# Moving chunk 0's block transposes of g into chunk 1, and batch 1's mask onto TensorE

## The chip, the cores and the metric

The kernel runs on one core of a Trainium2 chip. The metric is the device time of one execution in microseconds. Five engines work from their own in-order instruction streams: TensorE (PE; its weight loads are shown apart as PEld), VectorE (DVE), ScalarE (ACT), GpSimd (POOL) and SyncE (SP), which here issues every DMA.

## The reference, cut to what matters

```
attn  = softmax(mask(0.125 * q @ k^T)) @ v        # 4 batches x 8 heads x 576 tokens x 64
                                                  # heads 0-3: the last 32 positions; heads 4-7: every 32nd position
x     = attn as [2304, 512]
h     = x @ w_in                                  # w_in [512, 2048], stored as 64-bit floats
g     = h * sigmoid(1.702 * h)
x2    = g @ w_out                                 # w_out [2048, 512], stored as 64-bit floats
logits = x2 @ phi                                 # 32 slots
d     = softmax over tokens; slot_in = d^T @ x2
slot_out[e] = relu(slot_in[e] @ w1[e]) @ w2[e]    # 8 experts
out   = softmax over slots (logits) @ slot_out
```

## The kernel before

The 2304 tokens are worked in five chunks (four of 512, one of 256), each in 16 steps, one for each 128 columns of h. `moe_step(i)` writes step (c, f): it brings the weights on, advances the side work (the generators in `side`), issues block transposes of g, and calls `gemm1`, where twelve matmuls make h (L319), ACT makes tanh (L322) and DVE makes g (L323). g lies in slots of 512 columns: 19 in the tile `gT` and, from chunk 1 on, three more in `more`. The logits are taken from g every four steps (L338). At the chunk's end `post(c)` makes the softmax weights d and multiplies them with g (128 small matmuls, L433, result `us`). For that product g is needed with its 32x32 blocks transposed: `g_transpose` (L346, on DVE) reads a slot and writes into place f of `gT`, and `todo` lists what is still to be transposed.

Chunk 0 is different from the others: its 16 steps also bring in the weights. Each step converts two 512 KB tiles of 64-bit floats to 32 bits. `load_raw` (L248) fetches a tile into one of three `raw` buffers; ACT takes the absolute value (L259), POOL clamps (L260), DVE does three bit operations (L261, L262, L263), the last of which frees the buffer. `split` makes the two halves of a weight (ACT L270, POOL L271). For w_out there are also four PE transposes (L278), a store to a scratch (L275) and a product with phi (L288, L294).

The attention of batch 0 runs ahead of chunk 0. That of batch c+1 is side work of chunk c, one piece a step (two in step 0): `att_scores` (scores L161, mask, maximum L174, exponentials L179 with a sum each, L180 to L182), `att_transpose` and `att_values` (L216). For batch 0 (`early`) TensorE adds the mask into PSUM as a matmul with the identity (L154), and the maximum (L174, then a small multiply L176) and the exponentials read PSUM. For the other batches DVE adds the mask on the way from PSUM to SBUF (L164). Scores, weight transposes and most other small products share a pool of five PSUM tiles (`mtile`).

The program's text sets priorities only. A planner in the tile framework orders each engine's instructions ahead of the run, by what is ready in its own account; on the chip each engine then runs its list in order.

Of the kernel before, what the change touches and what calls it, by code (L numbers as in the profile page):

```python
# [30 lines left out]
NF = FF // 128  # L31
TFROM = 5
# [9 lines left out]
def tile_kernel(ctx: ExitStack, tc: tile.TileContext, lqk, lv, sqk, sv, wraw, phi, wexp, cst, out):  # L42
# [22 lines left out]
    def mtile(name):  # L65
        return ps_m.tile([P, 512], F32, tag="m", name=name)
# [61 lines left out]
    def att_scores(b, hp, part):  # L128
        t = qkv[b, hp]
        local = hp < 2  # L130
        nk, step = (KL, QT) if local else (KS, QS)
        ko = S if local else SW
        total, half = (NTL, 5) if local else (NTS, HS)
        u0, u1 = (0, half) if part == 0 else (half, total)
        nt = u1 - u0
        early = b == 0
        nm = f"{b}_{hp}_{part}"
        if part == 0:
            shape = [P, NTL if local else 2 * HS, nk]
            if b == 0 and hp >= 2:  # L140
                ts = ep.tile(shape, F32, name=f"ts_{b}_{hp}")
            else:
                ts = att.tile(shape, F32, tag="ts", name=f"ts_{b}_{hp}")
            probs[b, hp] = ts
            if not local:
                nc.gpsimd.memset(ts[:, NTS], 0.0)
        if local:
            ts = probs[b, hp][:, u0:u1]
        else:
            ts = probs[b, hp].rearrange("p (j e) k -> p e j k", e=2)[:, part, :nt]  # L150
        sp = mtile(f"s_{nm}")[:, :nt * nk].rearrange("p (u k) -> p u k", k=nk)
        mask = maskL if local else maskS
        if early:
            nc.tensor.matmul(sp, identb, mask.unsqueeze(1).to_broadcast([P, nt, nk]), start=True, stop=False)  # L154
            if local and part == 0:
                nc.tensor.matmul(sp[:, 0], identb, maskL0, start=False, stop=False)
        for u in range(nt):
            qo = step * (u0 + u)
            for h in range(2):
                hs = slice(64 * h, 64 * h + 64)  # L160
                nc.tensor.matmul(sp[hs, u], t[hs, qo:qo + 64], t[hs, ko + qo:ko + qo + nk], start=not early, stop=not early or u == nt - 1)  # L161

        def add_mask(a, z, m):
            nc.vector.scalar_tensor_tensor(ts[:, a:z], sp[:, a:z], SCALE, m.unsqueeze(1).to_broadcast([P, z - a, nk]), op0=ALU.mult, op1=ALU.add)  # L164

        if not early:
            if local and part == 0:
                add_mask(0, 1, maskL0)
                add_mask(1, nt, mask)
            else:  # L170
                add_mask(0, nt, mask)
        nmx = att.tile([P, 6], F32, tag="nmx", name=f"nmx_{nm}", bufs=4)
        src, sc = (sp, SCALE) if early else (ts, 1.0)
        nc.vector.tensor_reduce(nmx[:, :nt], src, axis=AX.X, op=ALU.max, negate=True)  # L174
        if early:
            nc.vector.tensor_scalar_mul(nmx[:, :nt], nmx[:, :nt], SCALE)  # L176
        sm = att.tile([P, 6], F32, tag="sm", name=f"sm_{nm}", bufs=4)
        for u in range(nt):
            nc.scalar.activation(ts[:, u], src[:, u], AF.Exp, scale=sc, bias=nmx[:, u:u + 1], accum_out=sm[:, u:u + 1])  # L179
        nc.vector.tensor_scalar_add(sm[:, :nt], sm[:, :nt], 1e-9)  # L180
        nc.vector.reciprocal(sm[:, :nt], sm[:, :nt])  # L181
        nc.gpsimd.tensor_tensor(ts, ts, sm[:, :nt].unsqueeze(2).to_broadcast([P, nt, nk]), op=ALU.mult)  # L182
# [68 lines left out]
    def load_w(f):  # L251
        for k in range(2):
            if (f, k) not in raws:
                load_raw(f, k)
        for k in range(2):
            raw = raws.pop((f, k))
            t = rawp.tile([P, 512], F32, tag="wc", name=f"wc_{f}_{k}", bufs=4)
            u = t.bitcast(U32)
            nc.scalar.activation(t, raw[:, :, 1].bitcast(F32), AF.Abs)  # L259
            nc.gpsimd.tensor_scalar(t, t, F64_LARGE, F64_SMALL, op0=ALU.min, op1=ALU.max)  # L260
            nc.vector.tensor_scalar(u, u, 3, 0x3FFFFFF8, op0=ALU.logical_shift_left, op1=ALU.bitwise_and)  # L261
            nc.vector.scalar_tensor_tensor(u, raw[:, :, 1], 0xC0000000, u, op0=ALU.bitwise_and, op1=ALU.bitwise_or)  # L262
            nc.vector.scalar_tensor_tensor(u, raw[:, :, 0], 29, u, op0=ALU.logical_shift_right, op1=ALU.bitwise_or)  # L263
            conv[f, k] = t

    def split(f):
        if f % 2 == 0:
            wis[f // 2] = wip.tile([P, 2, 2, 512], F32R, tag="wi", name=f"wi_{f // 2}")
        w, t = wis[f // 2][:, f % 2], conv.pop((f, 0))
        nc.scalar.copy(w[:, 0], t)  # L270
        nc.gpsimd.tensor_tensor(w[:, 1], t, w[:, 0].bitcast(F32), op=ALU.subtract)  # L271

    def wo_transpose(f):
        t = conv.pop((f, 1))
        nc.sync.dma_start(wo_scr[f], t)  # L275
        tp = mtile(f"wot_{f}")
        for kt in range(4):
            nc.tensor.transpose(tp[:, 128 * kt:128 * kt + 128], t[:, 128 * kt:128 * kt + 128], ident)  # L278
        woT[f] = rawp.tile([P, 4, 128], F32, tag="woT", name=f"woT_{f}", bufs=1)
        nc.scalar.copy(woT[f].rearrange("p k f -> p (k f)"), tp)  # L280
# [3 lines left out]
    def wo_phi(f):  # L284
        t = woT.pop(f)
        pw = mtile(f"wp_{f}")[:, :P]
        for kt in range(4):
            nc.tensor.matmul(pw[32 * kt:32 * kt + 32], phs[:, kt, :], t[:, kt, :], start=True, stop=True)  # L288
        wpT[f] = rawp.tile([P, P], F32, tag="wpT", name=f"wpT_{f}", bufs=2)
        nc.scalar.mul(wpT[f], pw, 0.5)  # L290

    def wo_phi_sum(f):
        pw = mtile(f"wq_{f}")[:, :NS]
        nc.tensor.matmul(pw, wpT.pop(f), sel, start=True, stop=True)  # L294
        nc.scalar.copy(wp[:, f, :], pw)  # L295
# [3 lines left out]
    slots, taken, where = {}, set(), {}  # L299

    def g_slot(c, f):
        k = next(k for k in [*range(NF, NF + 6), NF - 2, NF - 1] if k in slots and k not in taken)
        assert k >= NF or c == 0
        taken.add(k)
        where[c, f] = k
        return slots[k]
# [5 lines left out]
    def gemm1(c, f):  # L312
        N = CHUNKS[c][1]
        x, w = xt[c], wis[f // 2][:, f % 2]
        h = ps_h.tile([P, 512], F32, tag="h", name=f"h_{c}_{f}")
        n = 0
        for kt in range(4):
            for we, xe in ((0, 0), (0, 1), (1, 0)):
                nc.tensor.matmul(h[:, :N], w[:, we, 128 * kt:128 * kt + 128], x[xe][:, kt, :N], start=n == 0, stop=n == 11)  # L319
                n += 1  # L320
        g = g_slot(c, f)
        nc.scalar.activation(g[:, :N], h[:, :N], AF.Tanh, scale=0.851)  # L322
        nc.vector.scalar_tensor_tensor(g[:, :N], g[:, :N], 1.0, h[:, :N], op0=ALU.add, op1=ALU.mult)  # L323
        gs[c, f] = g
# [16 lines left out]
    def g_transpose(c, f):  # L341
        N = CHUNKS[c][1]
        if c < 4:
            assert f not in taken
            taken.add(f)
        nc.vector.transpose(t_slots(c)[:, f, :N], gs[c, f][:, :N])  # L346
        g_used(c, f)

    gt = []
    side, st, todo = [], {}, []  # L350

    def moe_step(i):
        c, f = steps[i]
        if i + 2 < NF:
            load_w(i + 2)
        if 0 < i < NF:
            wo_phi(i)
        if i <= NF and i:
            wo_phi_sum(i - 1)
        for s in list(side):  # L360
            if next(s, True):
                side.remove(s)
        if i + 1 < NF:
            split(i + 1)
        if c == 0 or f >= TFROM:
            for _ in range(1 if c == 0 else 2):
                if todo and (c or todo[0][1] not in taken):
                    g_transpose(*todo.pop(0))
        while todo and todo[0][0] < c and todo[0][1] not in taken:
            g_transpose(*todo.pop(0))  # L370
        gemm1(c, f)
        if i + 1 < NF:
            wo_transpose(i + 1)
        if i and f % 4 == 0:
            pc, pf = steps[i - 4]
            logits(pc, pf)
            if f == 0:
                side.append(post(pc))
        todo.append((c, f))

    def post(c):
        N = CHUNKS[c][1]
        ntt = N // 128
        first, last = c == 0, c == len(CHUNKS) - 1
# [35 lines left out]
        nc.scalar.copy(L[:, :ntt], lp[:, :N // 4].rearrange("p (t s) -> p t s", s=NS))  # L420
        st["L"] = L
        yield
        if not last:
            yield
        us = [mtile(f"u_{c}_{a}") for a in range(4)]
        nb = N // 32
# [1 line left out]
        for i in range(nb // 4):  # L428
            for a in range(4):
                for j in range(4):  # L430
                    b = 4 * i + j
# [141 lines left out]
    c = len(CHUNKS) - 1  # L573
# [4 lines left out]
    for _ in post(c):  # L578
        pass
# [148 lines left out]
    for half in range(1, len(COLS)):  # L728
        todo = list(PARTS)
# [75 lines left out]
```

## Time and profile before

| | us |
|---|---|
| Median of 3 runs (441.43 to 441.65) | 441.59 |
| Profiled execution, its own time | 442.75 |
| Span of the profiled execution | 441.0 |
| DVE busy in the span | 264.9 (60%) |
| PE busy in the span | 410.5 (93%) |
| ACT / POOL busy in the span | 195.3 (44%) / 78.5 (18%) |
| Chunk 0, from about 35 to 145 us | 110 |
| Chunk 1, from about 145 to 217 us | 72 |
| Chunk 2, from about 217 to 288 us | 71 |

Busy shares are means over stages that have different limits, and ends of matmuls are modelled, so a busy PE need not be a PE at its peak. The slices of the page (each digit is the busy share in tenths of one fortieth of the span) show DVE at 8 or 9 from slice 4 to slice 11, which is chunk 0, and at 4 to 6 after it. The granted TensorE clock is at full speed in all but the last slices.

### The profile page before, as it was taken

To read this page: it belongs to the slowest core of one execution; us is meant where nothing else is said; L and a number is where in the kernel's file an instruction comes from. 1 tells how busy PE (TensorE), PEld (TensorE's weight loads), DVE (VectorE), ACT (ScalarE), POOL (GpSimd) and SP (SyncE) were. 2 spreads that over 40 slices of the span, in tenths; PEclk is the share of its full clock that TensorE was granted. 3 is DMA by queue.
4 is the path that set the end of the run, shared out by engine and by line. 5 is a ranking of instruction groups with operands and counts; after the bars stand their busy time and mean duration, and the time that the engine had idled before them with its cause. 6 is when DMAs were issued, how large, how long until landed. Compare 5 with 4: busy or idle time off the path is not lost.

```text
span 441.0 us, 10075 instructions
## 1 busy us (share of the span) xinstructions
PE 410.5 (93%) x4082; PEld 282.8 (64%) x4088; DVE 264.9 (60%) x564; ACT 195.3 (44%) x639; POOL 78.5 (18%) x96
## 2 busy tenths in 40 slices
PE   8877898998989999999999999999999998999965
PEld 4555675655556767777676776776777795244654
DVE  2689999998987454565466535546454654431212
ACT  2785777766674644454543355321212222020312
POOL 0354445645540110100100001000000000000000
PEclk9999999999999999999999999999999999899995
DMA  8956757585663030221411101870003799779998
GB/s 245 358 164 221 248 177 278 182 310 180 223 199 113 9 100 2 91 81 52 153 42 58 38 2 36 283 289 1 1 0 143 291 387 349 271 305 424 426 355 251
DMA packets 25614, 80.90 MB, mean 183 GB/s; under 512 B 2144, under 2 KB 9440, under 8 KB 21472
## 3 DMA queue, kind: packets, MB, share of 16 engines
q1 hardware_dynamic: 25568, 80.26, 51.3%
q8 instruction: 32, 0.52, 0.5%
q14 instruction: 14, 0.11, 0.1%
HBM read 71.34 MB, written 8.91 MB: 182 GB/s over the span
## 4 chain that ended last, share of the span: by engine, by line
PE 67%; DVE 15%; ACT 6%; DMA 4%; POOL 4%; issue 3%; ACTq 0%; POOLq 0%
PE h L319 37%; PE u L433 5%; DMA out<-gT 4%; DVE wc L262 4%; PE lg L338 4%; PE s L161 3%; PE hp L637 3%; ACT ts L179 3%; DVE wc L263 3%; PE op L667 2%; PE ptp L197 2%; DVE wc L261 2%; PE av L216 2%; POOL wc L260 2%; PE busy L78 2%
## 5 line engine op out<-in xcount | busy, mean ns | idle before, releaser
L319 PE MATMUL h<-x,wi 128*128 128x512 f32 (+1 forms) x960 | 222.3, 379 | 1.2 <-DVE x L242 1.1
L319 PEld LDWEIGHTS h<-x,wi 128*128 128x128 f32 x960 | 161.8, 189 | 47.1 <-issue 13.8
L323 DVE SCALAR_TENSOR_TENSOR gT<-gT,h 128x512 f32<-128x512 f32 (+1 forms) x64 | 40.6, 634 | 62.2 <-ACT gT L322 61.6
L322 ACT ACTIVATE gT<-h 128x512 f32<-128x512 f32 (+1 forms) x64 | 35.5, 555 | 69.3 <-PE h L319 69.0
L179 ACT ACTIVATE ts<-ts,nmx 128x64 f32<-128x64 f32 (+1 forms) x120 | 41.6, 348 | 29.2 <-DVE nmx L174 28.9
L182 POOL TENSOR_TENSOR ts<-ts,sm 128x384 f32<-128x384 f32 (+2 forms) x32 | 28.6, 894 | 138.9 <-DVE sm L181 74.9
L346 DVE STREAM_TRANSPOSE gT<-gT 128x512 f32<-128x512 f32 (+1 forms) x64 | 41.0, 648 | 0.8
L260 POOL TENSOR_SCALAR wc<-wc 128x512 f32<-128x512 f32 x32 | 24.2, 759 | 29.1 <-ACT wc L259 29.1
L262 DVE SCALAR_TENSOR_TENSOR wc<-raw,wc 128x512 uint32<-128x512 uint32 x32 | 26.8, 839 | 0.3
L263 DVE SCALAR_TENSOR_TENSOR wc<-raw,wc 128x512 uint32<-128x512 uint32 x32 | 26.7, 835 | 0.2
L338 PE MATMUL lg<-gT,wp 128*32 128x512 f32 (+1 forms) x128 | 25.6, 564 | 0.7 <-ACT wp L295 0.6
L271 POOL TENSOR_TENSOR wi<-wc,wi 128x512 fp32r<-128x512 f32 x16 | 23.0, 1436 | 14.1 <-ACT wi L270 14.1
L197 PE MATMUL ptp<-cs,ts 128*96 128x128 f32 (+1 forms) x120 | 17.7, 280 | 8.4 <-POOL ts L182 7.7
L161 PE MATMUL s<-qk 64*64 64x96 f32 (+1 forms) x552 | 25.0, 236 | 0.2 <-DMA qk<-lqk 0.2
L161 PEld LDWEIGHTS s<-qk 64*64 64x64 f32 x552 | 20.9, 134 | 6.4 <-issue 4.9
L180 DVE TENSOR_SCALAR sm<-sm 128x5 f32<-128x5 f32 (+2 forms) x32 | 8.6, 268 | 26.7 <-ACT ts L179 26.7
L241 ACT CAST x<-av 128x320 fp32r<-128x320 f32 (+20 forms) x54 | 19.0, 396 | 10.8 <-DVE x L242 8.8
L197 PEld LDWEIGHTS ptp<-cs,ts 128*96 128x96 f32 (+1 forms) x120 | 12.8, 132 | 16.8 <-POOL ts L182 13.6
L433 PE MATMUL u<-gT,dT 32*32 32x512 f32 x576 | 21.5, 639 | 2.1 <-DVE z L408 2.1
L201 ACT COPY pt<-ptp 96x384 f32<-96x384 f32 (+1 forms) x34 | 14.9, 482 | 18.8 <-PE ptp L197 18.8
L261 DVE TENSOR_SCALAR wc<-wc 128x512 uint32<-128x512 uint32 x32 | 18.6, 584 | 7.2 <-POOL wc L260 7.1
L179 ACT ACTIVATION_READ_ACCUMULATOR ts<-ts,nmx 128x1 f32 x120 | 22.5, 187 | 0.0
(123 smaller groups left out, 467.8 us busy)
## 6 DMA issues: line engine op xcount, KB each, us to landing
ex<-wexp SPq DMA_DIRECT2D x28, 1024.0 KB, 7.8
raw<-wraw SPq DMA_DIRECT2D x32, 512.0 KB, 3.8
qk<-lqk SPq DMA_DIRECT2D x8, 592.0 KB, 4.8
wo_scr<-wc SPq DMA_DIRECT2D x16, 256.0 KB, 2.2
ex<-wo_scr SPq DMA_DIRECT2D x4, 1024.0 KB, 9.2
gT<-wexp SPq DMA_DIRECT2D x4, 1024.0 KB, 5.9
qk<-sqk SPq DMA_DIRECT2D x6, 604.0 KB, 4.2
v<-lv SPq DMA_DIRECT2D x8, 432.0 KB, 4.4
```

Of the source, the lines that this page charges most:

```text
L161: nc.tensor.matmul(sp[hs, u], t[hs, qo:qo + 64], t[hs, ko + qo:ko + qo + nk], start=not early, stop=not early or u == nt - 1)
L179: nc.scalar.activation(ts[:, u], src[:, u], AF.Exp, scale=sc, bias=nmx[:, u:u + 1], accum_out=sm[:, u:u + 1])
L197: nc.tensor.transpose(ptp[:nk, u - a], src, ident)
L260: nc.gpsimd.tensor_scalar(t, t, F64_LARGE, F64_SMALL, op0=ALU.min, op1=ALU.max)
L262: nc.vector.scalar_tensor_tensor(u, raw[:, :, 1], 0xC0000000, u, op0=ALU.bitwise_and, op1=ALU.bitwise_or)
L263: nc.vector.scalar_tensor_tensor(u, raw[:, :, 0], 29, u, op0=ALU.logical_shift_right, op1=ALU.bitwise_or)
L319: nc.tensor.matmul(h[:, :N], w[:, we, 128 * kt:128 * kt + 128], x[xe][:, kt, :N], start=n == 0, stop=n == 11)
L322: nc.scalar.activation(g[:, :N], h[:, :N], AF.Tanh, scale=0.851)
L323: nc.vector.scalar_tensor_tensor(g[:, :N], g[:, :N], 1.0, h[:, :N], op0=ALU.add, op1=ALU.mult)
L338: nc.tensor.matmul(lgs[c][32 * j:32 * j + 32, :N], wp[:, f0 + j, :], gs[c, f0 + j][:, :N], start=f0 == 0, stop=f0 == NF - 4)
L346: nc.vector.transpose(t_slots(c)[:, f, :N], gs[c, f][:, :N])
L433: nc.tensor.matmul(us[a][32 * j:32 * j + 32, :].rearrange("p (t f) -> p t f", f=32), dT[q, 32 * b:32 * b + 32], gT[q, :, 32 * b:32 * b + 3 ...
```

## The change

Four places change. Batch 1's scores take the mask on TensorE as batch 0's do. The g of chunk 0 goes into slot f + 3, and none of it is transposed in chunk 0. Its 16 transposes are issued in steps 0 to 3 of chunk 1, four a step, from slot f + 3 to place f; chunk 1's own transposes begin at step 6, not 5. `post(0)` waits two steps more before its product, which so comes in step 6 of chunk 1, not in step 4.

```diff
@@ att_scores
-        early = b == 0
+        early = b < 2
@@ g_slot
-        k = next(k for k in [*range(NF, NF + 6), NF - 2, NF - 1] if k in slots and k not in taken)
-        assert k >= NF or c == 0
+        if c == 0:
+            k = f + 3
+        else:
+            k = next(k for k in range(NF, NF + 6) if k not in taken)
@@ moe_step
-        if c == 0 or f >= TFROM:
-            for _ in range(1 if c == 0 else 2):
-                if todo and (c or todo[0][1] not in taken):
+        if c and f >= TFROM + (c == 1):
+            for _ in range(2):
+                if todo:
                     g_transpose(*todo.pop(0))
-        while todo and todo[0][0] < c and todo[0][1] not in taken:
+        while c and todo and todo[0][0] < c and (c > 1 or todo[0][1] < 4 * f + 4):
             g_transpose(*todo.pop(0))
@@ post
-        if not last:
+        for _ in range(3 if first else 0 if last else 1):
             yield
```

## Rows read from the trace of the kernel before

**Rows 1.** Windows: us, PE, PEld, DVE, ACT, POOL busy (instructions), clock, DMA share, GB/s.

```profile
42.00:133.00 91.00, 82.12 (x749) 55.60 (x749) 85.12 (x154) 65.52 (x198) 47.53 (x50) 1.00 0.66 223
```

**Rows 2.** Waits of queue SP, 42:133 us: us in total, times, longest.

```profile
SPq L248 <- DVE wc L263: 33.4, 12, 5.5
```

**Rows 3.** Timeline of SP (start, us): a load, three later, eighteen later.

```profile
56.43 0.33 SPq L248 DMA_DIRECT2D raw<-wraw  x1
...
65.18 0.37 SPq L248 DMA_DIRECT2D raw<-wraw  x1
...
117.82 0.33 SPq L248 DMA_DIRECT2D raw<-wraw  x1
```

**Rows 4.** DMA issues of the page: count, KB each, median us to landing.

```profile
raw<-wraw SPq DMA_DIRECT2D x32, 512.0 KB, 3.8
```

**Rows 5.** Timeline of one tile's conversion: ACT, then DVE's first and last operation.

```profile
60.13 0.68 ACT L259 ACTIVATE wc<-raw 128x512 f32<-128x512 f32 x1 [0.15 <-DMA raw<-wraw]
...
61.97 0.41 DVE L261 TENSOR_SCALAR wc<-wc 128x512 uint32<-128x512 uint32 x1
...
64.08 0.64 DVE L263 SCALAR_TENSOR_TENSOR wc<-raw,wc 128x512 uint32<-128x512 uint32 x1
```

**Rows 6.** Groups of DVE, 42 to 133 us: busy us, mean ns, idle before.

```profile
L263 DVE SCALAR_TENSOR_TENSOR wc<-raw,wc 128x512 uint32<-128x512 uint32 x26 | 22.6, 871 | 0.1
L262 DVE SCALAR_TENSOR_TENSOR wc<-raw,wc 128x512 uint32<-128x512 uint32 x27 | 21.4, 796 | 0.2
L261 DVE TENSOR_SCALAR wc<-wc 128x512 uint32<-128x512 uint32 x27 | 15.7, 584 | 4.3 <-POOL wc L260 4.2
L346 DVE STREAM_TRANSPOSE gT<-gT 128x512 f32<-128x512 f32 x14 | 9.8, 698 | 0.0
L323 DVE SCALAR_TENSOR_TENSOR gT<-gT,h 128x512 f32<-128x512 f32 x14 | 9.4, 674 | 0.3 <-ACT gT L322 0.3
L164 DVE SCALAR_TENSOR_TENSOR ts<-s,maskb 128x384 f32<-128x384 f32 (+2 forms) x10 | 4.6, 473 | 0.0
L174 DVE TENSOR_REDUCE nmx<-ts 128x5 f32<-128x480 f32 (+3 forms) x8 | 4.3, 551 | 0.0
L242 DVE TENSOR_TENSOR x<-av,x 128x128 fp32r<-128x128 f32 (+7 forms) x12 | 4.1, 345 | 0.9 <-ACT x L241 0.9
L180 DVE TENSOR_SCALAR sm<-sm 128x5 f32<-128x5 f32 (+2 forms) x8 | 3.2, 398 | 0.0
L181 DVE RECIPROCAL sm<-sm 128x5 f32<-128x5 f32 (+2 forms) x8 | 1.3, 168 | 0.0
```

**Rows 7.** Groups of 0 to 36 us: what batch 0's scores have beside them.

```profile
L154 PE MATMUL s<-maskb,identb 128*128 128x480 bf16 x2 | 0.7, 372 | 0.0
...
L176 DVE TENSOR_SCALAR nmx<-nmx 128x5 f32<-128x5 f32 x4 | 0.6, 157 | 0.1
```

**Rows 8.** Timeline, DVE and POOL at 53 us.

```profile
53.13 1.50 DVE L261 TENSOR_SCALAR wc<-wc 128x512 uint32<-128x512 uint32 x1 [0.27 <-POOL wc L260]
...
53.07 1.28 POOL L271 TENSOR_TENSOR wi<-wc,wi 128x512 fp32r<-128x512 f32 x1
```

**Rows 9.** Windows, the first four steps of chunk 1 (about).

```profile
145.00:159.00 14.00, 14.00 (x129) 10.82 (x127) 7.56 (x22) 7.97 (x26) 2.15 (x4) 1.00 0.12 33
```

**Rows 10.** Timeline of DVE behind chunk 0's product, step (1,4).

```profile
165.12 1.85 DVE L346 STREAM_TRANSPOSE gT<-gT 128x512 f32<-128x512 f32 x3
167.10 0.69 DVE L323 SCALAR_TENSOR_TENSOR more<-more,h 128x512 f32<-128x512 f32 x1
```

**Rows 11.** Timeline of one score tile to its last exponential, and a product.

```profile
104.09 0.91 PE L161 MATMUL s<-qk 64*64 64x64 f32 x24
...
105.59 0.55 DVE L164 SCALAR_TENSOR_TENSOR ts<-s,maskb 128x384 f32<-128x384 f32 x1
...
110.11 0.33 ACT L179 ACTIVATE ts<-ts,nmx 128x64 f32<-128x64 f32 x1
...
111.75 0.91 PE L216 MATMUL av<-pt,v 54*64 54x54 f32 x44
```

## The prediction

> **What bounds the kernel now.** I read the windows by stage first, then the waits and the timeline of the DMA queue, then the groups of DVE. Chunk 0 takes 110 us for 16 steps (6.9 a step); chunks 1 and 2 take 71 to 72 us for the same matmuls (4.5 a step), and there PE is busy all the time. So the change works in the one stage where PE isn't the limit. In the steady part of chunk 0, from 42 to 133 us, DVE is busy 85.1 of 91 us, 94%; ACT has 65.5, POOL 47.5 [rows 1]. PE's 82.1 is modelled and holds waits.
>
> What DVE holds up is seen in the queue that loads the weights: its commonest wait is a load of raw for L263, the DVE operation that frees one of three buffers [rows 2]. Load 11 is issued at 56.43, load 14 into the same buffer at 65.18, load 29 at 117.82 [rows 3]: 61.4 us for 18 loads is 3.41 us a load, and three times that, 10.2 us, a mean turn of one buffer. A turn has two halves. The load takes 3.8 us from issue to landing [rows 4], which no engine shortens. The conversion runs, for the tile loaded at 56.43, from ACT at 60.13 to the end of L263 at 64.72; of this DVE has it from 61.97, 2.75 us, with some 1.7 of its own work (0.41, 0.68 and 0.64) and 1.0 us of other DVE work put in between [rows 5]. The reader is to see a ring: load, ACT, POOL, DVE, next load. DVE is its busiest part, but 3.8 of 10.2 us is not DVE's at all.
>
> **The change part by part.** First, the transposes. 14 of chunk 0's 16 lie in that steady part, 9.8 us; two more lie behind it, where DVE has room. Then the mask: ten L164, 4.6 us, all of batch 1 [rows 6]. Added are eight small multiplies L176 at 0.157 us [rows 7], 1.3 us. Net 13.1 of the 96.4 us that the ten groups sum to; as neighbours overlap a little (96.4 summed against 85.1 busy), it is 13.1 x 0.88 = 11.6 us of DVE time.
>
> What is that worth? Upper end: DVE sets the pace, and all 11.6 us comes back. Lower end: the ring sets the pace, and only what stands between POOL's end and L263 counts. I take 1.0 to 1.5 us of foreign work a turn (1.0 in the turn shown; turns with a transpose inside have more). The weight operations are 59.7 of the 96.4 us, the foreign ones 36.7; 13.1 of 36.7 goes, 36%, so 0.36 to 0.54 us a turn. 26 loads are 8.7 turns: 3.1 to 4.7 us. The rows nearest to the question are the ring's, so I stay near that end: 5.5 us, a little above it, because exponentials and copies that queue on ACT ahead of a conversion wait for DVE too.
>
> One thing works against it. An L261 that takes 0.41 us in one place took 1.50 us at 53.13, beside POOL's L271 of 1.28 us [rows 5, 8]; the three weight operations have means of 0.58 to 0.87 us [rows 6] where the undisturbed ones have 0.41 to 0.68. The stretch is about 0.87 + 0.80 + 0.58 - 1.73 = 0.5 us a tile, 13 us over 26 tiles. With the foreign work thinned out, weight operations are 59.7 of 83.3 instead of 59.7 of 96.4 us, 16% more of DVE's time, and would meet POOL that much oftener: 2 us of the 11.6, 0.7 us in the ring. It is inside the choice of 5.5. The Trainium skill, SBUF — State Buffer, section Who interferes with whom, says that DVE and GpSimd share a pair of ports as an exclusive lock, and that a DVE instruction with at most one SBUF input outside the two-port modes doesn't contend. By it transposes and mask adds are work that POOL's operations can lie beside for nothing, and what stays is the work that POOL blocks; the trace agrees as far as the 14 transposes have a mean of 0.70 us [rows 6], no more than where POOL has little to do (three in 1.85 us, [rows 10]). By the rule alone up to 52% (POOL's 47.5 of 91) of the 11.6 us, 6 us, could come back as lock time, and the sum would fall to the ring's lower end.
>
> The g slots: in chunk 0 tanh no longer waits for a freed slot. I see no such wait of weight in the trace and put it at 0; one that I overlooked could only add to the gain.
>
> TensorE's mask costs eight matmuls of about 0.37 us or less [rows 7], under 3 us. In the steady part PE waits for the ring, which hides them; if PE became the limit of chunk 0 they'd cost up to 3 us, below nothing they can't go. I take 0. The exponentials read PSUM instead of SBUF; they lie on ACT, which has 25 us to spare in this stage [rows 1]; even 0.05 us more on each of the 40 would be 2 us there: 0.
>
> A score tile is held longer. The one at 104.09 is free when L164 ends at 106.14; after the change it is held until the last exponential, here about 110.4 [rows 11]. There are five such PSUM tiles; the fifth allocation behind this one is the product at 111.75. So the margin is about 1.3 us now and shrinks as steps get shorter. Where it runs out, PE stands in order with weight transposes and h behind it. Eight pieces at 0 to 1 us: 0 to 8 us, I take 0 to 0.5 within the 5.5.
>
> Then the first steps of chunk 1. 16 transposes at 0.62 us from start to start (three took 1.85 [rows 10]) are 9.9 us of DVE. Steps (1,0) to (1,3) are 14 us with DVE busy 7.6 and PE busy throughout [rows 9]; so 6.4 us is free; what lies free just before 145 I don't count. The planner may pull transposes ahead into gaps: it put three before the g of step (1,4), L323 at 167.10, though they stand behind it in the program [rows 10]. What is left over, up to 3.5 us, runs into steps 4 and 5, where the product no longer stands, since it waits until step 6. Nothing needs the transposes before that, but for slots 16, 17 and 18, which g takes again in steps 3 to 5. Delays: a mask, a maximum or a g of DVE behind a transpose, 0.6 us at a time; two h buffers hide most of it from PE. Bounds 0 and 3.5 us; I take 1.5. The product itself moves at no cost: same 128 matmuls, and chunk 1's transposes, two a step from step 6, are 20 places for 16.
>
> **Sum.** -5.5 + 1.5 = -4.0 us on a profiled time of 442.75 (span 441.0, 1.75 around it). That execution lies 1.16 above the median of the runs; the difference is carried over unchanged: 441.59 - 4.0 = 437.6. From chunk 1 on PE is the limit, and the tail's loads start by the buffers that PE frees, so a shift at chunk 0's end arrives at the end whole.
>
> **Rivals.**
> DVE sets the pace: 11.6 back, 1.5 lost: 431.5. For it: 94% busy. Against: every load sits directly behind L263 three tiles earlier, with 3.8 us of landing in the turn. Chance 0.20.
> The relief is hidden: the ring's load half and the lock eat it (the rule named above is one way), the ring gains 2 and chunk 1 loses 2 in full: 441.5, 0.13. For it: of one turn only 1.0 us is foreign.
> The other side: chunk 1's opening becomes DVE's. The 9.9 us don't fit in the gaps as they fall; the softmax of batch 2 waits behind transposes (mask, maximum, exponentials, sums in a chain), and PE, in order, stands at that transpose of probabilities. Or the same stand in chunk 0 at a held score tile. The place I price is chunk 1: six steps at 1 us and the tail of chunk 0 moving little, +6 - 3 = +3: 444.5. It decides once the loss a step is above 0.6 us (3.5 us over six steps). For it: DVE needs 7.6 + 9.9 = 17.5 us in steps that take 14. Against: the product is two steps later and the planner fills gaps. Chance 0.22.
> The forecast has 0.45, its own range is 434 to 440.5.
>
> **How the numbers follow.** What a measurement of this kernel can tell from no change is about 0.2%, 0.9 us: 440.7 to 442.5. Faster: 0.45 x 0.97 + 0.20 + 0.13 x 0.2 = 0.66. Same: 0.13 x 0.6 + 0.02 = 0.10. Slower: 0.22 + 0.13 x 0.2 = 0.24. The range 430 to 444 takes in the DVE end and most of the other side.
>
> **What would show it.** Right: loads of raw 3.2 us apart, not 3.41; chunk 0's end some 5 us earlier (the first tanh of chunk 1 near 140); no transpose before that; first L433 in step 6; PE still busy all through chunk 1, which is 1 to 2 us longer. Wrong: loads under 3.05 us apart (DVE set the pace), or unchanged (the load half did); PE idle in chunk 1's first six steps with probabilities as the releaser; PE waiting for exponentials in chunk 0.

## The result, and the profile after

The changed kernel takes 446.01 us (median of 14 runs, 443.13 to 449.54); the kernel before, run beside it, 442.69 (14 runs, 441.43 to 444.64). The ratio is 1.0092, interval 1.0071 to 1.0114: slower by 0.9%. The prediction, 437.6 with a range of 430 to 444, has the wrong sign. The profiled execution of after took 445.38 us with a span of 443.6, against 442.75 and 441.0.

**What was relieved.** The window 42 to 133 us of after (columns as in [rows 1]), then DVE's groups in it (busy us, mean ns, idle before):

```profile
42.00:133.00 91.00, 80.21 (x694) 53.74 (x694) 78.67 (x146) 60.55 (x191) 42.56 (x47) 0.98 0.65 218
```

```profile
L263 DVE SCALAR_TENSOR_TENSOR wc<-raw,wc 128x512 uint32<-128x512 uint32 x24 | 19.4, 813 | 0.2
L261 DVE TENSOR_SCALAR wc<-wc 128x512 uint32<-128x512 uint32 x25 | 14.5, 585 | 9.0 <-POOL wc L260 8.9
L348 DVE STREAM_TRANSPOSE gT<-gT 128x512 f32<-128x512 f32 x14 | 9.8, 702 | 0.3
...
L176 DVE TENSOR_SCALAR nmx<-nmx 128x5 f32<-128x5 f32 (+2 forms) x8 | 1.9, 235 | 0.0
```

DVE fell from 85.1 to 78.7 us of 91 [rows 1], but not by the part that was to bring most: L348, the transposes (L346 before), still stands with 14 instructions and 9.8 us, as in the row of before [rows 6]. L164 is gone, L176 has come. L261's idle time rose from 4.3 to 9.0 us: DVE has more room and waits for POOL. 3.7 of the 6.4 us are no relief at all: the weight operations (L261 to L263) fell from 59.7 to 56.0 us because fewer of them have come by 133 us.

**The transposes did not move.** The last two of them on DVE's timeline of after (start, us):

```profile
137.75 0.70 DVE L348 STREAM_TRANSPOSE gT<-gT 128x512 f32<-128x512 f32 x1
...
143.75 0.71 DVE L348 STREAM_TRANSPOSE gT<-gT 128x512 f32<-128x512 f32 x1
```

15 of chunk 0's 16 transposes start before the last tanh of chunk 0 (142.4 us), the first at 45.04. Before, it was 15 as well. In the program they stand in chunk 1; the planner put 13 of the 16 into DVE's list within 2 us of their g (the latest 8.1 us behind it), and pulled them ahead as it did with the three of [rows 10].

**What became late.** SP's loads in after, the same three as in [rows 3], and the last weight load (number 31) of after and of before:

```profile
58.36 0.33 SPq L248 DMA_DIRECT2D raw<-wraw  x1
...
69.01 0.38 SPq L248 DMA_DIRECT2D raw<-wraw  x1
...
123.14 0.33 SPq L248 DMA_DIRECT2D raw<-wraw  x1
...
130.41 0.33 SPq L248 DMA_DIRECT2D raw<-wraw  x1
```

```profile
124.71 0.33 SPq L248 DMA_DIRECT2D raw<-wraw  x1
```

The 18 loads take 64.8 us, 3.60 us a load against 3.41. Load 31 is 5.7 us later, and the first tanh of chunk 1 comes at 150.00 instead of 144.96 (before, then after):

```profile
144.96 0.57 ACT L322 ACTIVATE more<-h 128x512 f32<-128x512 f32 x1
...
150.00 0.57 ACT L324 ACTIVATE more<-h 128x512 f32<-128x512 f32 x1
```

The wait of the queue for L263 is 31.6 us instead of 33.4 [rows 2], so that row alone doesn't show the loss: it sums what the queue waited, not who was late in the ring.

ScalarE shows a place where a tile comes late. Its timeline at 45 us, first of before, then of after (start, duration; L259 is the absolute value that opens a tile's conversion, L179 an exponential of batch 1):

```profile
44.80 0.59 ACT L280 COPY woT<-wot 128x512 f32<-128x512 f32 x1 [1.23 <-PE wot L278]
45.28 0.69 ACT L259 ACTIVATE wc<-raw 128x512 f32<-128x512 f32 x1
46.37 0.38 ACT L179 ACTIVATE ts<-ts,nmx 128x96 f32<-128x96 f32 x1 [0.41 <-DVE nmx L174]
...
50.33 0.65 ACT L259 ACTIVATE wc<-raw 128x512 f32<-128x512 f32 x1
```

```profile
45.46 0.59 ACT L280 COPY woT<-wot 128x512 f32<-128x512 f32 x1 [2.00 <-PE wot L278]
45.94 0.35 ACT L179 ACTIVATE ts<-s,nmx 128x96 f32<-128x96 f32 x1
46.17 0.20 ACT L179 ACTIVATION_READ_ACCUMULATOR ts<-s,nmx 128x1 f32 x1
46.27 0.34 ACT L179 ACTIVATE ts<-s,nmx 128x96 f32<-128x96 f32 x1
...
48.48 0.39 ACT L179 ACTIVATE ts<-s,nmx 128x96 f32<-128x96 f32 x1
48.71 0.25 ACT L179 ACTIVATION_READ_ACCUMULATOR ts<-s,nmx 128x1 f32 x1
48.80 0.71 ACT L259 ACTIVATE wc<-raw 128x512 f32<-128x512 f32 x1
...
52.81 1.27 ACT L259 ACTIVATE wc<-raw 128x512 f32<-128x512 f32 x2
```

The tile of L259 was loaded at 40.28 (after) and 40.38 (before) and landed 3.5 us later in both. Before, its L259 starts at 45.28, ahead of the nine exponentials. In after the nine stand first, 45.94 to 48.8, and L259 starts at 48.80, 3.5 us later (2.9 us of it are the exponentials); the next tile's starts at 52.81 instead of 50.33. Over tiles 6 to 31, exponentials run for 7.6 us between a tile's landing and its L259, against 3.1 us before (summed from the two traces).

Why the order changed: before, a score piece passed through the mask L164, the maximum and then the exponentials; now it goes from TensorE straight to the maximum. In the planner's account the exponentials are ready earlier and take ScalarE's turn first. That is inferred from the two lists. How much of the loss this order is, e6, e8 and e12 below bear on, but none of them isolates it.

**The clock.** PE's granted clock in 40 slices, of before and of after (row 2 of the page):

```profile
PEclk9999999999999999999999999999999999899995
```

```profile
PEclk9999999899999999999999999999999999999995
```

In after the digit 8 in the eighth slice is a stretch at half of the full clock:

```profile
70.00:77.60 7.60, 5.29 (x40) 4.19 (x37) 7.08 (x13) 4.98 (x18) 3.56 (x5) 1.00 0.64 206
77.60:81.00 3.40, 3.40 (x16) 1.92 (x15) 2.44 (x4) 1.26 (x3) 1.13 (x2) 0.50 0.40 148
```

Ahead of it PE was busy for 5.29 of 7.6 us (6.28 in the same window of before, with the clock full). Before has a like stretch only in the tail, 374.7 to 378.1 us, which after hasn't; there the lead of 5.0 us that before has at chunk 0's end (4.4 still at the tanh of step (4,15)) shrinks to the 2.6 us between the two spans; 3.4 us at half can cost 1.7. Over the 14 runs of after the time follows the mean clock (correlation -0.92, 2.85 us for 0.01 of clock); the median clock is 0.980, against 0.981 to 0.983 in the runs of before beside the experiments. By that slope up to 1 of the 3.3 us between the medians is clock.

### The profile page after: what moved, and what is told of

Same layout as the page of the kernel before. It is cut to its first block, busy times and chain, and to the rows that moved or that the text cites. A ratio compares the mean times of both kernels' runs of the same rounds, so it can differ in the third digit from the quotient of the medians.

```text
span 443.6 us, 10098 instructions
## 1 busy us (share of the span) xinstructions
PE 411.7 (93%) x4098; PEld 283.1 (64%) x4098; DVE 262.5 (59%) x562; ACT 193.4 (44%) x639; POOL 76.1 (17%) x96
## 4 chain that ended last, share of the span: by engine, by line
PE 68%; DVE 11%; ACT 6%; DMA 6%; POOL 4%; issue 4%; ACTq 0%; POOLq 0%; DVEq 0%; SPq 0%
PE h L321 38%; PE u L435 4%; DMA out<-gT 4%; PE s L161 4%; PE lg L340 4%; PE hp L639 3%; DVE wc L262 3%; ACT ts L179 3%; PE op L669 2%; DMA raw<-wraw 2%; PE ptp L197 2%; PE av L216 2%; POOL wi L271 2%; PE busy L78 2%; DVE wc L263 1%
## 5 line engine op out<-in xcount | busy, mean ns | idle before, releaser
L325 DVE SCALAR_TENSOR_TENSOR gT<-gT,h 128x512 f32<-128x512 f32 (+1 forms) x62 | 39.3, 633 | 59.3 <-ACT gT L324 58.6
L324 ACT ACTIVATE gT<-h 128x512 f32<-128x512 f32 (+1 forms) x62 | 34.5, 556 | 69.2 <-PE h L321 69.0
L348 DVE STREAM_TRANSPOSE gT<-gT 128x512 f32<-128x512 f32 (+1 forms) x62 | 39.7, 649 | 1.1
L179 ACT ACTIVATE ts<-ts,nmx 128x64 f32<-128x64 f32 (+1 forms) x80 | 27.7, 348 | 25.6 <-DVE nmx L174 25.3
L262 DVE SCALAR_TENSOR_TENSOR wc<-raw,wc 128x512 uint32<-128x512 uint32 x32 | 29.3, 917 | 0.3
L260 POOL TENSOR_SCALAR wc<-wc 128x512 f32<-128x512 f32 x32 | 23.2, 729 | 35.3 <-ACT wc L259 34.1
L179 ACT ACTIVATE ts<-s,nmx 128x64 f32<-128x64 f32 (+1 forms) x80 | 24.9, 340 | 4.0 <-DVE nmx L176 3.7
L261 DVE TENSOR_SCALAR wc<-wc 128x512 uint32<-128x512 uint32 x32 | 18.3, 575 | 11.9 <-POOL wc L260 11.8
L259 ACT ACTIVATE wc<-raw 128x512 f32<-128x512 f32 x32 | 21.7, 684 | 8.2 <-DMA raw<-wraw 7.1
L263 DVE SCALAR_TENSOR_TENSOR wc<-raw,wc 128x512 uint32<-128x512 uint32 x32 | 25.0, 784 | 0.2
L340 PE MATMUL lg<-gT,wp 128*32 128x512 f32 (+1 forms) x124 | 24.3, 563 | 0.5 <-ACT wp L295 0.5
L180 DVE TENSOR_SCALAR sm<-sm 128x5 f32<-128x5 f32 (+2 forms) x32 | 7.0, 220 | 27.9 <-ACT ts L179 27.9
L435 PE MATMUL u<-gT,dT 32*32 32x512 f32 x576 | 20.2, 597 | 2.1 <-DVE z L410 2.1
```

What stands on the lines that cost most here:

```text
L340: nc.tensor.matmul(lgs[c][32 * j:32 * j + 32, :N], wp[:, f0 + j, :], gs[c, f0 + j][:, :N], start=f0 == 0, stop=f0 == NF - 4)
L435: nc.tensor.matmul(us[a][32 * j:32 * j + 32, :].rearrange("p (t f) -> p t f", f=32), dT[q, 32 * b:32 * b + 32], gT[q, :, 32 * b:32 * b + 3 ...
```

## The experiments

My theory after the result: the mask edit loses by ScalarE's order, and the move of the transposes does nothing, because the planner undoes it. Rivals: the held score tiles, the later product, the new slots, the clock. Each ratio below has the kernel before, run beside it, as its base (medians 442.4 to 443.0).

**e1, the mask alone.** On the kernel before:

```diff
-        early = b == 0
+        early = b < 2
```

> The kernel before with batch 1's mask on TensorE and nothing else. Theory A (the whole loss is the mask edit: with the mask added by TensorE the planner finds batch 1's exponentials ready earlier and puts them on ScalarE ahead of the absolute values of the weight tiles, so the three-buffer ring of loads turns more slowly): as slow as the full change, +2.5 to +4.5 us, first tanh of chunk 1 near 150 us, loads of raw about 3.6 us apart. Theory B (the slots three apart and the later product cost the time): within 1 us of before, or faster by the 4 us of VectorE time that the mask adds took.

446.88 us, ratio 1.0105 (1.007 to 1.0139). One condition loses as much as the whole change. Its L259 at the place shown above starts at 49.42 and load 31 at 131.28. In its profile the clock is at half from 101.2 to 108.0 us, and the median clock of its runs is 0.976, against 0.983 of before's beside it.

**e2, all but the mask.** The change with `early = b == 0`.

> The full change without the mask edit (batch 1's mask on VectorE again). Theory A: the planner still puts chunk 0's transposes into chunk 0, so nothing has moved; within 1 us of before, first tanh of chunk 1 near 145 us. Theory B: +3 to +5 us.

444.25 us, 1.0039 (1.0021 to 1.0058). 15 transposes still lie in chunk 0, from 51.27 us on. So the text moved, the work did not, and the kernel is 0.4% slower. In its profile load 14 is 0.4 us later than before's and load 18 2.2 us; between them, from 75.4 to 78.8 us, the clock is at half.

**e3, the transposes really moved; e4, the same with the mask.** e2 (e4: after) with each transpose of chunk 0 tied behind a g of the step before the one where it is issued:

```diff
+        if c == 0:
+            p = NF - 1 + f // 4
+            tc.add_manual_dep(t, gmade[steps[p]], ..., reason="held back")
```

> As the run without the mask edit, with an order edge that holds each transpose of chunk 0 behind the g of the step before the one it is written in, so that the 16 really lie in chunk 1. The ring estimate of the prediction: chunk 0 3 to 5 us shorter, chunk 1 1.5 us longer (at most 3.5), total -2 to -4 us. If VectorE sets the pace: chunk 0 about 9 us shorter, total -7 us. If chunk 1's opening becomes VectorE's: total above +1 us, with PE idle in chunk 1's first six steps.

> The full change with the same order edge: the transposes lie in chunk 1 and the mask is on TensorE. Theory A: the loss of the mask edit (+2.5 to +4.5 us) stands beside the gain of the held transposes (-2 to -4): -1 to +2 us. If VectorE time is what counts in chunk 0, both edits add up: -7 us or better.

e3: 442.6 us, 1.0008 (0.9981 to 1.0034). e4: 445.23, 1.007 (1.0043 to 1.0096). In e3 no transpose lies in chunk 0. Its window of chunk 0, the first 14 us of its chunk 1, and the clock:

```profile
42.00:133.00 91.00, 82.18 (x687) 55.33 (x686) 73.59 (x137) 61.81 (x191) 44.20 (x48) 0.94 0.66 223
...
148.40:162.40 14.00, 14.00 (x127) 10.89 (x125) 13.53 (x28) 7.63 (x25) 2.80 (x4) 1.00 0.13 33
```

```profile
PEclk9999999999599999999999999999999999899985
```

DVE has 73.6 of 91 us, 11.5 less than before, as much as I had forecast for both edits together, and the time is the same. Most of it turned up as DVE's wait for POOL ahead of L261, 14.1 us instead of 4.3 [rows 6]:

```profile
L261 DVE TENSOR_SCALAR wc<-wc 128x512 uint32<-128x512 uint32 x26 | 15.4, 594 | 14.1 <-POOL wc L260 14.1
```

In chunk 1's opening DVE is busy 13.53 of 14 us and PE still 14.00: the 16 transposes cost nothing there, and (1,0) to (2,0) takes 71.5 us as before. The clock was at half for 10.2 us (112.6 to 122.8), and a gain can hide under that: over e3's runs the time follows the mean clock (correlation -0.97, 2.7 us for 0.01), and their median clock is 0.977 against 0.983 of before's, worth some 1.6 us by that slope. e2, the same kernel with the transposes still in chunk 0, takes 1.65 us more than e3. So, as an estimate, moving them is worth 1 to 2 us where the clock doesn't take it back; e7, at full clock in chunk 0 but with more matmuls, shows nothing. e4 loses 0.7% with the transposes out of the way: the mask costs without them too.

**e5, the transposes left out.** e2 with chunk 0's transposes not done (slots 0 to 2 set to zero).

```diff
-        nc.vector.transpose(t_slots(c)[:, f, :N], gs[c, f][:, :N])
+        if c:
+            nc.vector.transpose(t_slots(c)[:, f, :N], gs[c, f][:, :N])
```

> Chunk 0's 16 transposes are left out altogether (the product of chunk 0 reads its g untransposed); otherwise the run without the mask edit. An upper bound of what moving them can give. If VectorE time in chunk 0 is worth what the prediction said: raw loads 3.2 us apart or less, first tanh of chunk 1 at 140 us, -4 to -9 us. Theory A (the ring is held by load latency and by the fixed order on each engine, so VectorE relief is worth little): first tanh of chunk 1 within 2 us of before's 145 us in an execution without a half-clock stretch, total -3 to +1 us.

441.74 us, 0.9981 (0.9957 to 1.0006). With the work gone for good, and no half clock in chunk 0, the first tanh of chunk 1 comes at 144.1, 0.9 us earlier than before. The nearer base is e2, of which e5 is an edit: 2.5 us less (444.25 to 441.74), of which e2's 3.4 us at half clock can be up to 1.7. So 16 transposes are worth some 0.9 to 2.5 us; the prediction's 3.1 to 4.7 for both edits gives the transposes 2.3 to 3.5 (9.8 of 13.1), and its 5.5 gives them 4.1.

**e6, the mask alone with L259 first; e12, the whole change with L259 first.**

```diff
-            nc.scalar.activation(t, raw[:, :, 1].bitcast(F32), AF.Abs)
+            with tc.high_priority():
+                nc.scalar.activation(t, raw[:, :, 1].bitcast(F32), AF.Abs)
```

> The mask edit alone, with the absolute values of the weight tiles given priority over the exponentials in the planner. Theory A (the loss of the mask edit is the order on ScalarE): most of the +4.4 us of the mask edit goes, to +1 us or below, and the absolute value of load 7 again starts near 45 us. If the loss is the mask's own work on TensorE or the longer hold of the PSUM tile: still +3 us or more.

> The full change with the absolute values given priority in the planner, nothing else. Theory A (the loss is the order on ScalarE that the mask edit brings): 441.5 to 443.5 us. If the moved transposes' slots and the later product have a loss of their own, as the run without the mask edit hints: 443.5 to 445 us.

e6: 442.21 us, 0.9981 (0.9965 to 0.9997), 4.7 us under e1. e12: 443.47, 1.0004 (0.9983 to 1.0026), 2.5 us under after. ScalarE in e6 at the same place (L260 is L259 here):

```profile
43.62 0.66 ACT L260 ACTIVATE wc<-raw 128x512 f32<-128x512 f32 x1
44.19 0.33 ACT L179 ACTIVATE ts<-s,nmx 128x96 f32<-128x96 f32 x1
...
45.45 0.36 ACT L179 ACTIVATE ts<-s,nmx 128x96 f32<-128x96 f32 x1
45.67 0.22 ACT L179 ACTIVATION_READ_ACCUMULATOR ts<-s,nmx 128x1 f32 x1
46.37 0.67 ACT L260 ACTIVATE wc<-raw 128x512 f32<-128x512 f32 x1 [0.48 <-issue]
46.95 0.32 ACT L179 ACTIVATE ts<-s,nmx 128x96 f32<-128x96 f32 x1
```

The exponentials are still early, but the first tile stands ahead of all nine (L260 at 43.62) and the next behind the fifth (46.37). Between a tile's landing and its L260 exponentials run for 3.9 us in all. The same instructions in another order recover the whole loss, clock included (median 0.983, as before's).

That does not yet show that the order was what lost it. L259 first also pays where the mask edit changes nothing: load 6, ahead of every exponential of batch 1, goes out 3.2 us earlier than in before, because L259 there overtakes exponentials of batch 0 (e6, then before):

```profile
34.33 0.38 SPq L248 DMA_DIRECT2D raw<-wraw  x1
...
37.58 0.37 SPq L248 DMA_DIRECT2D raw<-wraw  x1
```

By load 14 e6 is still 2.0 us ahead of before, by load 31 1.4 us behind it. In e12 load 6 is 3.2 us ahead of after's, load 31 2.8 us. So the rival that L259 first has a gain of its own, beside a loss of the mask that goes on, is open; the kernel before with L259 first would tell, and was not run. Against the other rivals the traces speak: no wait of PE for L179 stands among those of 42 to 133 us in after, e1 or e6 (held score tiles), and the 40 exponentials take less time from PSUM (12.5 us in after, 13.9 in before).

**e7 and e8, the clock.** e3 and after, each with one more `keep_busy` matmul (a product whose result is not used) in each step of chunk 0 from the second on and one in each group of weight transposes from the third on, so that PE has fewer gaps.

> The held transposes without the mask edit, and two idle-filling matmuls a step in chunk 0 (some 0.2 us each), one ahead of h and one ahead of the weight transposes. If half-clock stretches in chunk 0 eat the gain of the held transposes: none of them in the profile, runs within 1 us of each other, 439.5 to 441.5 us. If the matmuls cost what they take on TensorE: +5 us against the held version.

> The full change with the same idle-filling matmuls. If the clock is the main part of the loss: at or below before's 442.5 us. Theory A (order on ScalarE is the main part, the clock 1 to 2 us of it): 443 to 445 us, without a half-clock stretch in chunk 0.

e7: 442.5 us, 0.9994 (0.997 to 1.0018). e8: 444.96, 1.0045 (1.0028 to 1.0062). The clock of chunk 0 is full in both (e8's window 42 to 133: 1.00 against 0.98 in after). So of the loss of 0.92% about half (0.47 points) goes with the half-clock stretches, though the matmuls also shift the order, and e7 gains nothing by them. That the half clock is itself a consequence, by gaps that the late ring leaves on PE, fits e1 and e6 but is argued. In e8 the L259 of the place shown above still starts at 48.86, behind the nine exponentials, and yet load 16 is level with before's (73.63 against 73.60): the delay there can be made up, so this place alone doesn't carry the loss.

**e9 and e10, a fourth buffer.** Both are built on e2, with the transposes written in chunk 1. In e10 chunk 0's g goes into slots 0 to 15 and is transposed in place, so `gT` shrinks to 17 slots (`more` grows to 5) and a fourth `raw` buffer fits. Nothing is left out; the mask stays on VectorE. e9 is e10 with chunk 0's transposes left out.

```diff
-        raw = rawp.tile([P, 512, 2], U32, tag="raw", name=f"raw_{f}_{k}")
+        raw = rawp.tile([P, 512, 2], U32, tag="raw", name=f"raw_{f}_{k}", bufs=4)
...
+        if c == 0:
+            k = f
```

> Chunk 0's transposes left out as before, g of chunk 0 in slots 0 to 15, and the memory so freed holds a fourth buffer for the weight loads. If the three-buffer ring holds chunk 0 (load latency in the turn), a fourth buffer lets the next limit show: raw loads 2.9 to 3.2 us apart, first tanh of chunk 1 at 133 to 139 us, total 431 to 437 us. If the fixed order of the engines holds it: within 1.5 us of the run without transposes (441.7).

> Nothing left out: g of chunk 0 lies in slots 0 to 15 and is transposed in place, a fourth buffer for the weight loads, batch 1's mask on VectorE. If the ring was the limit: a gain, smaller than without transposes, 434 to 440 us; VectorE then over 95% busy in chunk 0. If not: 441 to 444 us.

e9: 438.0 us, 0.9878 (0.9845 to 0.9912). e10: **434.53, 0.981 (0.9773 to 0.9848)**, faster than both kernels. The window of e10 and its load 31:

```profile
42.00:133.00 91.00, 82.28 (x774) 58.68 (x772) 86.36 (x159) 66.19 (x207) 46.66 (x49) 1.00 0.69 232
```

```profile
113.25 0.37 SPq L248 DMA_DIRECT2D raw<-wraw  x1
```

Load 31 goes out 11.5 us earlier than before and the first tanh of chunk 1 comes at 138.1. DVE is busier than before (86.36 of 91), with 12 transposes of chunk 0 still in it. It wasn't at its limit at 85.1. e9, with less work for DVE and the same buffers, is slower than e10 (its clock in the window is 0.98, e10's 1.00).

**e11, e10 with the mask on TensorE and L259 first.**

> As the run with transposes in place and four buffers, with the mask on TensorE and the absolute values given priority. If VectorE becomes the limit once the ring is longer, its 4.6 us of mask adds now count: 2 to 4 us below the run with the mask on VectorE. If not: the same within 1 us.

439.94 us, 0.9924 (0.9897 to 0.9951), 5.4 us over e10. In its profile the clock is at half in four stretches of chunk 0 (mean 0.94 from 42 to 133). Exponentials ahead of L259 don't explain it: they run for 5.9 us between landings and L259, against 8.6 in e10. So with L259 first a kernel with the mask on TensorE can still be the slower one. Its median clock is 0.973 against 0.983 of e10, by the slope of after's runs some 3 of the 5.4 us; why the clock falls oftener there isn't settled.

**e13, the control: e10 with three buffers.**

> The kernel of e10 (g of chunk 0 in slots 0 to 15, transposed in place, mask on VectorE) with three raw buffers instead of four; everything else equal. If the fourth buffer is what won, the loads fall back to 3.4 to 3.5 us apart, the first tanh of chunk 1 to 143 to 147 us, and the time is 442 to 445 us, 8 to 10 us above e10. If the slots in place (and the order that the planner makes of them) won, loads stay 3.2 us apart and the time stays within 2 us of 434.5. Mine: 443.

444.1 us, 1.0039 (1.0012 to 1.0065), 9.6 us over e10. Load 31:

```profile
126.64 0.33 SPq L248 DMA_DIRECT2D raw<-wraw  x1
```

The gain of e10 is the buffer, with the order that the planner makes for it; e13, with the slots in place and three buffers, loses 0.4%, as e2 does. Its profile has the clock at half from 99.5 to 102.9 us, at most 1.7 of the 9.6 us.

**e14, the later product alone; e15, the slots f + 3 alone**, each on the kernel before.

```diff
-        if not last:
+        for _ in range(3 if first else 0 if last else 1):
             yield
```

> One part of the change alone, on the kernel before: the product of chunk 0 (L433) waits two steps more, and chunk 1's own transposes begin at step 6. The mask, the slots and the transposes stay as before. Chunk 0 holds nothing of it, so the first tanh of chunk 1 should stay at 145.0, load 31 at 124.7. If the product's place costs nothing: 442 to 443 us (ratio 0.998 to 1.002). If it is what e2 lost (0.39%): 444 to 445.

> Another part alone, on the kernel before: the g of chunk 0 goes into slot f + 3; its transposes stay issued in chunk 0, the product in step 4. With e14 it splits the 0.39% that e2 lost. If the slots (and the planner's order behind them) lose it: 444 to 445 us, with load 31 later than 126 us. If they lose nothing: within 0.2% of before, 442 to 443.5. Mine: 444, since e2's load 31 was 2.6 us late while its chunk 1 took no longer.

e14: 443.01 us, 0.9999 (0.9981 to 1.0017). e15: 441.84, 0.9993 (0.997 to 1.0017), against my 444. Neither loses. What is left of e2's edits is the transposes' later place in the text, and with it their priority: they are still done in chunk 0, but at other points of DVE's list (72.0 and 73.3 us where before has 64.8 and 70.4). e13 has that too. Part of the 0.4% is clock; the rest is put down to this order by exclusion only, and no run has e14's and e15's edits together without it.

## Why the prediction was wrong

- **What bounds chunk 0.** I read the ring of three buffers as a rival to DVE and took a value near the ring's end. The ring was what bound it: e10 against e13 shows it. "DVE sets the pace" falls, with 94% busy.
- **The transposes, "what is that worth?": this step failed twice.** They weren't moved (15 in chunk 0 before and after). I cited the planner's reordering in [rows 10] for chunk 1's opening and did not ask what it does to chunk 0, nor make it a rival. And the term was mis-sized: of the 5.5 us 4.1 are the transposes'; doing without them measured 0.9 us against before and 2.5 against e2 (e5), and moving them nothing against before, 1.65 us against e2 (e3), part of both being clock. What stands between two operations on DVE is not lost to the ring if the ring then waits for POOL, ScalarE or the landing: L261's idle time, 4.3 us before [rows 6], is 9.0 in after and 14.1 in e3.
- **The mask on TensorE, taken as 4.6 us of DVE work saved with everything else at 0: the step that turned the sign.** Alone it costs 4.4 us (e1). The likeliest place is the exponentials at 0, since "they lie on ACT, which has 25 us to spare in this stage". Their own time was right: 40 take 12.5 us in after and 13.9 before. But a spare 25 us is a sum over the stage, and ScalarE opens every turn of the ring with L259: nine exponentials put ahead of one L259 delay that turn by 3.5 us, and with L259 first e1's loss is gone (e6, 4.7 us under e1). By the slope of after's runs some 2 of these are clock (0.976 against 0.983), and L259 first has a gain of its own, of unknown size at the end. That the mask costs is shown; that it costs by this order is argued.
- **The mask's matmuls at 0, the held score tile at 0 to 0.5, the g slots at 0, the product's move at 0.** Nothing speaks against them: e14 and e15 are no slower than before (upper ends 0.17%), and in after no wait of PE for L179 stands among the waits of 42 to 133 us. The matmuls were not run apart. The eight L176 took 1.9 us, not 1.3.
- **DVE's contention with POOL.** L261 and L348 have the same means as before (585 and 702 ns; 584 and 698 in [rows 6]); L262 rose from 796 to 887 and L263 fell from 871 to 813, so the three weight operations take 2.29 us a tile instead of 2.25. Hardly more of it came. e3, with the transposes gone from chunk 0, is no slower than before, so a loss by meeting POOL oftener doesn't show. The Trainium skill, SBUF — State Buffer, section Who interferes with whom, calls the ports that DVE and GpSimd share an exclusive lock; whether some of the relief went there, no run here separates.
- **Chunk 1's opening, +1.5 (0 to 3.5), and the rival of 444.5.** The rival of 444.5 is nearest to the measured time by luck, not by its place: after's opening is as long as before's, (1,0) to (2,0) 71.0 us against 71.5. The mechanism is refuted where it was really tried: DVE at 13.53 of 14 us and PE without a gap (e3).
- **"a shift at chunk 0's end arrives at the end whole".** In the two profiles 5.0 became 2.6 us, with a half-clock stretch in the tail of before alone. Up to (4,15) 4.4 arrived.

## What to carry to other kernels

Where a planner orders the engines' lists, look in the trace for whether a moved instruction moved, and whether an edit that only shortens one chain lets it overtake another. Setting the priority of the operation that opens the next turn of a bounding ring by hand is worth a try (e6 and e12 gained by it), with a control that has the priority alone. An engine at 94% in a stage need not be its bound where transfers wait for a buffer; try one more buffer first. Taking work out of a busy engine in a ring is worth only what the ring doesn't then spend waiting for somebody else.

## What was not expected of the hardware

The granted clock of TensorE fell to half (1.2 of 2.4 GHz) in the middle of chunk 0, for 3.4 us in after and 10.2 us in e3. In the 7.6 us ahead of it PE was busy for 5.29 us (after) and 6.05 us (e3, below):

```profile
105.00:112.60 7.60, 6.05 (x72) 3.72 (x70) 7.53 (x14) 5.80 (x21) 2.93 (x4) 1.00 0.55 176
112.60:122.80 10.20, 9.12 (x48) 6.43 (x50) 8.46 (x16) 4.70 (x12) 5.56 (x6) 0.50 0.77 242
```

How much of a run falls under it differs between runs of one kernel: e3's 12 runs go from 439.72 us (mean clock 0.989) to 445.47 (0.970). In this kernel a difference of 0.5% can be clock alone, so the mean clock of each run has to be read beside its time.
